# Weight slabs of the last two groups: asked for on ScalarE's queue instead of SyncE's

## The chip, the cores and the metric

The kernel runs on one core of a Trainium2 chip. Its time is the device time of one execution in microseconds (us). The time before is 1066.16 us, the median of 3 runs (1065.87 to 1067.72).

Engines go by their short names: PE is TensorE (matmuls; PEld its weight loads), DVE VectorE, ACT ScalarE, POOL GpSimd, SP SyncE. SP does no arithmetic here: it only sends out DMA transfers. ACT and POOL can send out transfers too, in order with their other work.

## The reference

Two blocks follow each other. All is fp32, with batch 8, 8 heads, 576 tokens and head size 64, so a row has 512 numbers.

```python
# attention inside chunks of 64 tokens
scores = (1 / sqrt(64)) * q_c @ k_c.T
attn = exp(scores - max(scores)); attn = attn / (sum(attn) + 1e-9)
x = attn @ v_c                        # then heads joined: (8, 576, 512)
# mixing by a Fourier transform over tokens and over columns, then an MLP
u  = x + real(fft(fft(x, axis=1), axis=2))
un = (u - mean(u)) / sqrt(var(u) + 1e-6)
out = u + relu(un @ w_ch1) @ w_ch2    # 512 -> 2048 -> 512
```

## The kernel before, in words

**Groups.** The 4608 rows (8 batches of 576) make 36 tiles of 128 rows, and the MLP takes them four at a time: nine groups, 0 to 8. Attention and the Fourier mixing of the next batch are woven into the MLP of the running group. Group 8 holds the four tiles with what is left of each batch, and has no attention beside it. `mlp(g)` runs the first product (512 to 2048, "up") and then the second one (2048 to 512, "down").

**Fewer multiplications.** From group 1 on the products are done by schemes that trade multiplications for sums. `up_halves` works on a pair of 128-column blocks of the result at a time, four pairs a group. A pair takes seven turns instead of eight, each one a smaller product of the weights' sums with the rows' sums; a turn is eight matmuls of 128x256, for two blocks r = 0 and 1. The turns follow `UP`. What becomes of a turn's result in PSUM (banks `pa` and `pb`) is written behind it: ACT copies the second turn's result (L1306) and DVE adds it to the first (L1307); DVE adds others (L1309, L1313, L1319, L1322); ACT applies the relu (L1317, L1320, L1323).

**The second product of the last two groups.** `down_few` (groups 7 and 8) has a list `PRODUCTS` of 26 small products, eight matmuls L1419 each, in place of 32. POOL sums operands between them (L1199, in `sums`), DVE adds results to the output rows (L1429).

**Weights.** The sums of weights are made once and kept in scratch tensors in HBM: `s1` for the first product, `s2` and `s3` for the second. From there they come back as slabs. A first-weight slab is 256 KB and goes to one of ten places in `wa` (`slab1`). A second-weight slab of `down_few` is 512 KB and goes to one of ten places (`slab3`): six in `wb`, two in rows of `xall` that are no longer needed, two in tiles called `more`. The contents of `s3` are made while group 6 ends and group 7 begins: the generator `make_rest` loads parts (L1137), POOL and DVE add them (L1148), and SP stores the results (L1155).

**Who asks for a slab, and when.** `fetch(which)` sends out the next slab of its kind, counted by `n_slab`. In the kernel before all go through SP's queue. First-weight slabs (L1171): ten ahead, and then one behind each turn of `up_halves`, into the place that this turn has just read; so the transfer waits for that turn's matmuls. The 28 slabs of a group (four pairs of seven) are asked for ten turns ahead of their use: in group 7 its slabs 10 to 27 and group 8's first ten, in group 8 the last 18. Second-weight slabs of groups 7 and 8 (L1174): in group 7 the first ten at fixed steps of the first product, as their places and contents come free (the `count` line in the main loop), and then one behind each small product. SP's queue also holds `make_rest`'s loads and stores and the stores of output rows (L1054; the low tiles go through POOL's queue, L1043).

**Order.** Each engine works its instructions off in order. The framework deals eight completion semaphores in turn to all transfers that SP and ACT send out, in the order in which it schedules them, and lets a transfer wait until the one that had the semaphore before it has landed.

Of the kernel before, what the change touches and what calls it, by code (L numbers as in the profile page):

```python
# [16 lines left out]
def kernel(  # L17
# [32 lines left out]
    nc = tc.nc  # L50
# [52 lines left out]
    NO, HF = 7, KF // 2  # L103
    UP = (1, 0, 2, 3, 4, 6, 5)
    s1 = dram.tile([HF // 2, NO, 128, 2 * 2 * 128], FP32, name="s1")
    s2 = dram.tile([NO, 128, HF * HM], FP32, name="s2")
    NS1, NS2, Z1, Z2 = 10, 3, 2 * 2 * 128, HF * HM
    slab1 = [wa[:, i * Z1:(i + 1) * Z1].rearrange("p (k r f) -> p k r f", r=2, k=2) for i in range(NS1)]
# [11 lines left out]
    PRODUCTS = (  # L120
        ("a41", "b11", "c", "+41", "a41=a22+a42 a22=a21-a22 a21=a41-a21"),
        ("a44", "b42", "b", "+42", "a44=a24+a44 a31=a21+a31"),
        ("y0", "s8", "d", "+12", ""),
        ("y3", "s21", "c", "+31+32+42", "y3=a43-y3"),
        ("y1", "s0", "d", "+11+21", "y1=a44-y1 y1=y1-a23 y0=a12-y0"),
        ("a22", "sb22", "f", "-22", "a22=a32-a34 a32=a42-a32"),
        ("a23", "s19", "d", "+22", ""),
        ("a44", "s15", "b", "+41", ""),
# [26 lines left out]
    NR2, NS3 = len(PRODUCTS), 10  # L155
# [952 lines left out]
    def block_of(name):  # L1108

        if name[0] == "s":  # L1110
            return s3[STORED.index(name)]
        o, k = (2, "dw".index(name)) if name in "dw" else ({"b1": 0, "b2": 0, "b3": 4 + "12".index(name[2]), "b4": 4 + "12".index(name[2])}[name[:2]], (int(name[1]) - 1) % 2)
        return s2[o, :, k * Z3:(k + 1) * Z3]
# [49 lines left out]
    FEW = NG - 2  # L1163
# [3 lines left out]
    def fetch(which):  # L1167
        i = n_slab[which]
        if which == 1 and i < HF // 2 * NO * (NG - 2):
            pair, o = divmod(i % (HF // 2 * NO), NO)  # L1170
            nc.sync.dma_start(out=slab1[i % NS1].rearrange("p k r f -> p (k r f)"), in_=s1[pair, UP[o]])  # L1171
        elif which == 3 and i < NR2 * (NG - FEW):
            to = slab3[i % NS3].rearrange("p m e -> p (m e)")
            nc.sync.dma_start(out=to, in_=block_of(PRODUCTS[i % NR2][1]))  # L1174
        elif which == 2 and i < NO * (FEW - first_of[2]):
            nc.sync.dma_start(out=slab2[i % NS2].rearrange("p m e -> p (m e)"), in_=s2[i % NO])
        n_slab[which] = i + 1
# [102 lines left out]
    def up_halves(g):  # L1280
# [4 lines left out]
        for pair in range(HF // 2):  # L1285
            pas, pbs = {}, {}
            for turn_, o in enumerate(UP):
# [36 lines left out]
                if g > 1:  # L1324
                    fetch(1)
# [7 lines left out]
    def down_halves(g, h1):  # L1333
        pas, pbs = {}, {}
        for o in range(NO):
            w = slab2[((g - first_of[2]) * NO + o) % NS2]
            for r in range(2):
# [45 lines left out]
                if r == 1:  # L1383
                    if o == 1:
                        for j in range(0, HF, 2):
                            two = ys[:, j:j + 2]
                            nc.gpsimd.tensor_tensor(
                                out=two, in0=h1[:, HF + j:HF + j + 2, lo], in1=two, op=ALU.subtract
                            )
                    if o == 2:  # L1390
                        for i in range(2):
                            nc.gpsimd.tensor_tensor(
                                out=os_[:, 2 * i + 1, HM:DM], in0=tmp[:, i, 0],
                                in1=natural(groups[g][2 + i])[:, HM:DM], op=ALU.add,
                            )
                    fetch(2)
                yield

    def down_few(g, h1):
# [3 lines left out]
        for o, (a, _, bank, reads, then) in enumerate(PRODUCTS):  # L1403
# [19 lines left out]
            for sign_, i, j in zip(reads[0::3], reads[1::3], reads[2::3]):  # L1423
# [7 lines left out]
                if left[i] == 0:  # L1431
                    store(n, os_[:, i])
            sums(h1, then.split())
            fetch(3)
            if o % 2 == 0:
                continue
# [14 lines left out]
    with tc.manual_schedule():  # L1451
# [79 lines left out]
        for g in range(NG):  # L1531
            for _ in mlp(g):
# [51 lines left out]
                for _ in range(2 if t > begin[1] else 0):  # L1584
                    if put_off:
                        b, t0_, r, o = put_off.pop(0)
# [60 lines left out]
```

## Time and profile before

| | |
|---|---|
| median of 3 runs | 1066.16 us (1065.87 to 1067.72) |
| profiled execution | 1065.92 us |
| its span, first to last instruction | 1064.1 us |
| PE busy | 1043.1 us (98%) |
| DVE, POOL, ACT busy | 627.6, 433.3, 314.9 us |
| first product of group 7 begins (PE) | 868.67 us |
| second product of group 7 begins | 917.86 us |
| first product of group 8 begins | 966.52 us |
| second product of group 8 begins, PE ends | 1015.0, 1059.9 us |
| SP's waits for PE ahead of L1171 and L1174, whole run | 81.7 + 42.3 and 49.6 us |

Times inside the profile count from the span's start. A timeline row gives the start, the duration, engine, line and operation, what it writes and reads, the shapes and how many instructions it joins; in brackets stands how long the engine was idle before it and what ended that. "SPq" and "ACTq" are transfers being sent out; their duration is that of the sending, not of the transfer. A row of the chain of waits that begins with DMA gives the time from sending to landing. The clock that the throttle granted to PE was 0.998 of full speed over the span.

### The profile page before, as it was taken

Reading aid. Unit: us, or ns where it says so; the run is one execution under the profiler, and the core shown is the slowest. Engines: PE = TensorE matmul, PEld = TensorE weight load, DVE = VectorE, ACT = ScalarE, POOL = GpSimd, SP = SyncE. Lnnn points to the kernel's source line nnn. Section 1 sums busy time; section 2 is a strip of 40 time slices with the busy share of each in tenths; the row PEclk is TensorE's granted clock in tenths of the full one; section 3 lists DMA queues with packets and bytes.
Section 4 is the critical chain, followed back from the end, with each engine's and each line's share of the span. In section 5 each row is a group of like instructions: output and inputs, shape, how many; then the busy total and the mean of one; then the engine's idle time right before and its main releaser. Section 6 shows DMA issues by size and latency. Waiting matters only on the chain.

```text
span 1064.1 us, 20223 instructions
## 1 busy us (share of the span) xinstructions
PE 1043.1 (98%) x7482; PEld 852.0 (80%) x7482; DVE 627.6 (59%) x1339; ACT 314.9 (30%) x744; POOL 433.3 (41%) x555
## 2 busy tenths in 40 slices
PE   8999998899999999999999999999999999999998
PEld 6645454788888888888888888888888888888887
DVE  4798987774567465664565645745664666433332
ACT  4688563233113311332022312331133102101210
POOL 4310018753425151244134421614251777650282
PEclk9999999999999999999999999999999999999999
DMA  8767575778478447973687359944753759998364
GB/s 178 223 199 215 146 217 199 208 231 294 161 217 238 128 146 213 242 211 111 186 235 212 113 170 231 246 132 159 228 158 103 271 174 356 348 407 280 90 213 143
DMA packets 167088, 219.10 MB, mean 206 GB/s; under 512 B 77228, under 2 KB 111020, under 8 KB 161614
## 3 DMA queue, kind: packets, MB, share of 16 engines
q1 hardware_dynamic: 155978, 211.98, 64.3%
q0 software_dynamic: 9024, 4.91, 2.1%
q8 instruction: 60, 0.98, 0.4%
q10 hardware_dynamic: 1988, 0.92, 0.3%
q14 instruction: 38, 0.31, 0.1%
HBM read 183.61 MB, written 34.08 MB: 205 GB/s over the span
## 4 chain that ended last, share of the span: by engine, by line
PE 79%; DVE 7%; ACT 4%; DMA 4%; SPq 3%; issue 1%; POOL 1%; ACTq 0%; DVEq 0%; POOLq 0%
PE pa L1301 20%; PE pb L1355 15%; PE pb L1301 15%; PE pa L1355 12%; PE dn L1419 7%; PE pt L399 2%; PE mix L839 2%; PE z L722 1%; PE xp L501 1%; SPq L265 1%; PE sc L451 1%; DMA s<-part 1%; DMA xall<-in_moe_w_ch_dram 1%; DVE power L380 1%; DMA more<-s 1%
## 5 line engine op out<-in xcount | busy, mean ns | idle before, releaser
L1301 PE MATMUL pa<-unT,wa 128*128 128x256 f32 x736 | 175.1, 381 | 0.0
L1301 PEld LDWEIGHTS pa<-unT,wa 128*128 128x128 f32 x736 | 138.1, 190 | 19.4 <-DVE h L1319 0.4
L1301 PE MATMUL pb<-wa 128*128 128x256 f32 x448 | 106.6, 381 | 0.0
L1301 PEld LDWEIGHTS pb<-wa 128*128 128x128 f32 x448 | 84.3, 190 | 11.5
L1355 PE MATMUL pa<-wb,h 128*128 128x256 f32 x384 | 87.2, 380 | 0.0
L1355 PE MATMUL pb<-wb,h 128*128 128x256 f32 x384 | 86.4, 379 | 0.0
L1185 POOL TENSOR_TENSOR h<-h 128x256 f32<-128x256 f32 x48 | 40.8, 857 | 101.2 <-DVE wb L1183 91.7
L1355 PEld LDWEIGHTS pa<-wb,h 128*128 128x128 f32 x384 | 71.8, 190 | 9.7
L1355 PEld LDWEIGHTS pb<-wb,h 128*128 128x128 f32 x384 | 72.0, 190 | 9.4
L1043 POOL DMA_DIRECT2D out_dram<-wb x28 | 18.8, 674 | 122.8 <-DVE wb L1372 71.9
L1307 DVE TENSOR_TENSOR wa<-pb,wa 128x256 f32<-128x256 f32 x56 | 23.7, 424 | 63.1 <-ACT wa L1306 63.1
L1301 PE MATMUL pb<-unT,wa 128*128 128x256 f32 x256 | 60.6, 379 | 0.3 <-DVE wa L1307 0.3
L1317 ACT ACTIVATE h<-pa 128x256 f32<-128x256 f32 x64 | 24.5, 383 | 114.8 <-PE pa L1301 114.3
L1252 PE MATMUL dn<-wb,h 128*128 128x512 f32 x128 | 57.4, 596 | 0.0
L1306 ACT COPY wa<-pa 128x256 f32<-128x256 f32 x56 | 20.8, 372 | 121.2 <-PE pa L1301 121.2
L1301 PEld LDWEIGHTS pb<-unT,wa 128*128 128x128 f32 x256 | 48.6, 190 | 7.2 <-DVE wa L1307 0.7
L1199 POOL TENSOR_TENSOR h<-h 128x512 f32<-128x512 f32 x34 | 43.0, 1280 | 27.1 <-ACT h L1323 23.9
L1301 PE MATMUL pa<-wa 128*128 128x256 f32 x224 | 53.9, 383 | 0.0
L1323 ACT ACTIVATE h<-h 128x512 f32<-128x512 f32 x64 | 39.8, 629 | 42.6 <-DVE h L1322 42.2
L483 ACT COPY pT<-pt 128x512 f32<-128x512 f32 x36 | 20.9, 581 | 105.8 <-PE pt L399 105.5
L1211 PE MATMUL up<-unT,wa 128*128 128x512 f32 x108 | 49.4, 598 | 0.0
L856 POOL TENSOR_TENSOR xall<-y,xall 128x513 f32<-128x513 f32 x14 | 22.7, 1620 | 62.3 <-DVE y L850 48.1
(312 smaller groups left out, 2139.6 us busy)
## 6 DMA issues: line engine op xcount, KB each, us to landing
wa<-s SPq DMA_DIRECT2D x196, 256.0 KB
wb<-s SPq DMA_DIRECT2D x42, 1024.0 KB
wb<-s SPq DMA_DIRECT2D x32, 512.0 KB
xall<-in_moe_w_ch_dram SPq DMA_DIRECT2D x22, 512.0 KB
q<-in_q_dram SPq DMA_DIRECT2D x96, 112.0 KB
k<-in_k_dram SPq DMA_DIRECT2D x96, 112.0 KB
s<-part SPq DMA_DIRECT2D x32, 256.0 KB
v<-in_v_dram SPq DMA_DIRECT2D x124, 64.0 KB
```

Source lines behind the costliest of these rows:

```text
L399: nc.tensor.transpose(pt[:, j, :], src(j), ident)
L856: eng.tensor_tensor(out=x[:, 0:w], in0=y[:, 0:w], in1=x[:, 0:w], op=ALU.add)
L1185: nc.gpsimd.tensor_tensor(out=h1[:, m, hi], in0=h1[:, m, lo], in1=h1[:, m, hi], op=ALU.subtract)
L1199: eng.tensor_tensor(out=out_, in0=a, in1=b, op=op)
L1211: nc.tensor.matmul(out=up, lhsT=w1[:, kk, m * 128:(m + 1) * 128], rhs=unT[:, kk], start=(kk == 0), stop=(kk == KD - 1), skip_group_check=True,
L1252: nc.tensor.matmul(out=dn, lhsT=h1[:, m, s * 128:(s + 1) * 128], rhs=w2[:, m, :], start=(m == 0), stop=(m == KF - 1),)
L1301: nc.tensor.matmul(out=dst, lhsT=w[:, kk, r], rhs=rhs[o][:, kk], start=(o in (0, 1) and kk == 0), stop=(kk == 1), skip_group_check=True,)
L1307: nc.vector.tensor_tensor(out=b, in0=pbs[r][:, 0], in1=a, op=ALU.add)
L1317: nc.scalar.activation(out=h1[:, m, lo], in_=dst, func=ACTF.Relu)
L1323: nc.scalar.activation(out=h1[:, HF + m], in_=h1[:, HF + m], func=ACTF.Relu)
L1355: nc.tensor.matmul(out=dst, lhsT=lhs[:, m], rhs=w[:, m], start=(o in (0, 2) and m == 0), stop=(m == HF - 1), skip_group_check=True,)
L1419: nc.tensor.matmul(out=dst, lhsT=lhs[:, m], rhs=w[:, m], start=(fresh and not half and m == 0), stop=(m == 3), skip_group_check=True,)
```

## The change

Which engine sends out a slab now depends on its number. First-weight slabs from number 150 on go through ACT's queue (`HF // 2 * NO * (FEW - 2) + NS1` is 28 x 5 + 10): that is each one asked for from the first turn of group 7 on, 46 in all. Second-weight slabs from number 10 on go through ACT's queue too, 42 in all; the first ten, those asked for during group 7's first product, stay with SP. Each `fetch` stands at the same place in the program, so ACT sends a slab out between the copies and activations that are written before and after it. The semaphores are dealt anew, as the scheduler now orders two queues.

```diff
         i = n_slab[which]
         if which == 1 and i < HF // 2 * NO * (NG - 2):
             pair, o = divmod(i % (HF // 2 * NO), NO)
-            nc.sync.dma_start(out=slab1[i % NS1].rearrange("p k r f -> p (k r f)"), in_=s1[pair, UP[o]])
+            eng = nc.scalar if i >= HF // 2 * NO * (FEW - 2) + NS1 else nc.sync
+            eng.dma_start(out=slab1[i % NS1].rearrange("p k r f -> p (k r f)"), in_=s1[pair, UP[o]])
         elif which == 3 and i < NR2 * (NG - FEW):
             to = slab3[i % NS3].rearrange("p m e -> p (m e)")
-            nc.sync.dma_start(out=to, in_=block_of(PRODUCTS[i % NR2][1]))
+            eng = nc.scalar if i >= NS3 else nc.sync
+            eng.dma_start(out=to, in_=block_of(PRODUCTS[i % NR2][1]))
```

## The prediction

> **What bounds the kernel now.** I read the busy times first, then the waits of each engine, then stretches of the last 250 us.
>
> ```profile
> PE 1043.1 (98%) x7482; PEld 852.0 (80%) x7482; DVE 627.6 (59%) x1339; ACT 314.9 (30%) x744; POOL 433.3 (41%) x555
> ```
>
> TensorE (PE) is busy for 98% of the span: 21 us of idle time in all, most of it in the opening. Up to group 7 (its first product begins at 868.67 us) the two programs stand in the same order, so only what follows can change. The stretches (length, then PE, PEld, DVE, ACT, POOL busy, clock, share of the DMA engines, GB/s):
>
> ```profile
> 872.00:876.00 4.00, 3.71 (x18) 2.97 (x17) 3.67 (x6) 0.37 (x1) 1.36 (x2) 1.00 0.46 138
> 875.00:935.00 60.00, 59.02 (x271) 50.71 (x269) 32.84 (x63) 13.26 (x30) 41.67 (x31) 1.00 0.96 350
> 905.00:910.00 5.00, 4.98 (x24) 4.07 (x23) 4.55 (x7) 1.63 (x5) 4.32 (x3) 1.00 0.71 264
> 910.00:915.00 5.00, 5.00 (x25) 4.41 (x24) 1.95 (x5) 0.77 (x2) 0.09 (x1) 1.00 0.82 258
> 920.00:925.00 5.00, 5.00 (x25) 4.38 (x24) 1.08 (x4) 0.00 (x0) 4.84 (x4) 1.00 1.04 404
> 967.00:1015.00 48.00, 48.00 (x224) 42.27 (x223) 16.70 (x40) 13.86 (x31) 9.40 (x10) 1.00 0.44 133
> 1015.00:1060.00 45.00, 44.92 (x209) 39.20 (x207) 12.14 (x31) 0.56 (x2) 26.86 (x22) 1.00 0.61 202
> ```
>
> Group 8 (967 to 1060) leaves nothing to win: PE full, DMA half empty. The only late weights are in group 7, whose 60 us run the DMA engines at 0.96. Its second product, PE alone in order of time:
>
> ```profile
> 926.50 1.89 PE L1419 MATMUL dn<-wb,h 128*128 128x256 f32 x8
> 928.38 3.69 PE L1419 MATMUL dn<-xall,h 128*128 128x256 f32 x16
> 932.11 1.97 PE L1419 MATMUL dn<-more,h 128*128 128x256 f32 x8
> 935.22 1.97 PE L1419 MATMUL dn<-more,yall 128*128 128x256 f32 x8 [1.15 <-DMA more<-s]
> 937.06 1.97 PE L1419 MATMUL dn<-wb,yall 128*128 128x256 f32 x8
> ```
>
> Eight matmuls make one small product, and where nothing is late one follows another every 1.727 us. From 926.50 to 937.06 there are five, 8.63 us of work in 10.56: PE loses **1.93 us** to slabs 6 to 10, of which the wait view books 1.15. Why they are late is seen in the chain of waits and in SyncE's (SP's) order of time:
>
> ```profile
> 913.78 5.91 DMA s<-part
> 919.75 6.93 DMA s<-part
> 928.09 6.99 DMA more<-s
> ```
> ```profile
> 869.33 5.30 SPq L1054 DMA_DIRECT2D out_dram<-wb  x4
> 877.18 0.90 SPq L1171 DMA_DIRECT2D wa<-s  x2
> 879.11 1.83 SPq L1171 DMA_DIRECT2D wa<-s  x2
> 881.26 3.37 SPq L1155 DMA_DIRECT2D s<-part  x4
> ```
>
> One queue holds the first-weight slabs (L1171), the stores of sums that POOL is making (L1155) and the second-weight slabs (L1174). The fetch that PE releases at 870.4 goes out at 877.18, behind stores. Fetch 27 is released at 917.9 and goes out at 928.6. Slab 9, the last of those that stay on SP, goes out at 928.09 and lands 6.99 us later.
>
> **The change, part by part.** 88 transfers leave SP for ScalarE (ACT): 28 first-weight fetches in group 7's first product, 18 in group 8's, 26 second-weight fetches in group 7's second product, 16 in group 8's. Nothing is added or dropped on PE, DVE or POOL. Semaphores matter, though. Eight are dealt in turn to every transfer of SP and ACT, and a transfer first waits until the one eight before it has landed. SP's transfers now wait for ACT's and the reverse; the engine stands in order behind each wait.
>
> *SP's queue.* In 869 to 929 it loses 28 issues of 0.375 us (median of L1171), 10.5 us, and their waits for PE. Stores and slabs move up. How far, the DMA engines decide: idle are about 2.2 us in 872 to 876, and 1.45 + 0.9 us in 905 to 915. So slabs 6 to 10 can land about 4.5 us earlier. They need 1.9 us at most: the loss goes, **-1.9 us**. Bounds: 0 (the queue is no faster) and -1.93. What is late next is DVE's L1307, which holds PE for 0.29 us at 874.31 and stays. The rows speak against more: at a share of 1.04 a second queue brings no bytes. The Trainium skill (DMA: Bandwidth & Descriptors, Issuing engines are not separate DMA queues) goes further: transfers of all issuers share 16 engines, so a second issuer saves its issue time alone. Taken strictly it leaves the slabs late and the sum 1.9 us higher. The idle shares, 0.71 and 0.82 ahead of the slabs, are why I don't follow it that far.
>
> *ACT's queue in group 7.* 28 x 0.375 + 26 x 0.32 us (medians) is 19 us of issuing on an engine that is busy for 13.26 of 60 us: beside other work. What counts is which ACT work stands behind a held fetch. In every pair of blocks (seven turns of 1.73 us) it is the copy L1306:
>
> ```profile
> 883.04 1.89 PE L1301 MATMUL pa<-unT,wa 128*128 128x256 f32 x8
> 884.11 0.37 ACT L1306 COPY wa<-pa 128x256 f32<-128x256 f32 x1 [1.64 <-PE pa L1301]
> 884.77 1.89 PE L1301 MATMUL pa<-wa 128*128 128x256 f32 x8
> ```
>
> The next turn writes the PSUM tile that this copy reads and waits for it. The copy ends at 884.48, PE goes on at 884.77: 0.29 us of slack, no more. The fetch ahead of it is released at about 883.2, so it may end as late as 884.4. Of the four pairs:
> - Pair 0 (fetch 0): the transfer eight before has long landed, so only the issue counts, 0.32 to 1.88 us (fastest and slowest L1171). At the slow end the copy ends at 872.8, PE starts late by 0.7 us and gets 0.45 back, as it stood for L1307. 0 to 0.3; I take 0.2, as SP's four stores at 869.33 took 1.3 us each.
> - Pair 1: fetch 7 waits for the first of the four stores at 881.26. With the four fetches (2.73 us) gone from ahead of it that goes out at 878.5, lands 4.6 (the landing there, by the semaphore's updates) to 6.99 us later, 883.1 to 885.5. 0 to 1.5; I take 0.4, nearer the landing at that place.
> - Pair 2: fetch 14 waits for fetch 10, which ACT sends out at 890 to 891 (fetch 10 itself waits for fetch 7, out at 884) and which lands 5 to 7 us later, 895 to 898, against 896.1 that is in time. 0 to 1.9; I take 0.6.
> - Pair 3: fetch 21 waits for fetch 18, out at about 903.5, through the emptier stretch of 905 to 915: 908 to 910 against 908.4. 0 to 2.0; I take 0.3.
>
> Together **+1.5 us**, between 0 and 4.5 (a late pair makes the next less late, so the four ends don't add). The other ACT work has room: in pair 1 the first activation L1317 ends at 889.67 and PE wants its tile at 891.68, and no matmul of this product waits for L1320 or L1323. On the first fetch the Trainium skill has a harsher rule (Perfetto Trace Analysis, DMA Instruction — HWDGE): the descriptor generator is shared and locked, and the profiled issue contains the wait for it. Behind SP's store of 869.33 to 871.40 and one of 2.1 us, pair 0 would cost about 1.4 us in place of 0.2, the sum 1.2 us more; only the start, where both queues issued together, hints at it in the rows.
>
> *Group 7's second product.* ACT has two copies L1012 there, 20.55 and 14.05 us idle before them; the fetch ahead of each waits for a product that PE has left behind. Cover 14 us: 0. POOL's out stores have a queue of their own and pass nothing.
>
> *Group 8.* A transfer eight back is eight turns old, 13.8 us, against landings of 2 to 4 us; fetches are not held, and 0.375 us ends before the copy. 0; should the slow issue (1.88) fall ahead of a copy, 0.4 us. In its second product ACT is busy for 0.56 of 45 us: 0. The closing stores stay where they were: 0.
>
> Sum: 1065.92 (profiled execution; span 1064.1, 1.8 around it) - 1.9 + 1.5 = 1065.5. The median of the runs is 0.24 above that execution: **1065.8 us**, no change that shows, as 0.2% (2.1 us) is about what a measurement of this kernel can tell from none.
>
> **Rivals.**
> 1. *ACT becomes the gate* (slower). If landings stay at 6 to 7 us right through 880 to 912, pairs 1 to 3 each hold the copy by more than 1 us, PE stops four times in group 7, and DVE's adds behind the copy delay the sums that POOL stores, which the next fetch waits for. Upper end 4.5 us, and more with that loop: 1066.2 - 1.9 + 4.5 to 6 = 1068.8 to 1070.3. For it: share 1.01 to 1.06 in 885 to 905 and 0.29 us of slack. Against: SP's stores go out earlier. It decides from 4.0 us of copy delay.
> 2. *All slabs early, no copy held* (the most that can be won): 1066.2 - 1.9 - 0.2 = 1064.1. For it: the scheduler spreads the eight semaphores anew. Against: rows of 5.9 to 7.0 us.
> 3. *Slabs 6 to 10 stay late*: bytes bound group 7, nothing is won, copies cost 1.5: 1067.7. For it: 0.96 over 60 us. Against: 0.71 and 0.82 before the slabs.
>
> **How the numbers follow.** Forecast 0.52 (1064.6 to 1067.0), ACT as gate 0.26, full gain 0.12, slabs still late 0.10. Faster by over 0.2% needs below 1064.0: half of the full gain, 0.06. Slower needs above 1068.3: nearly all of the first rival and a third of the third, 0.28. The rest, 0.66, is within. The range goes from the full gain, 1064.0, to the upper part of the first rival, 1070.0.
>
> **What would show it.** Right: no wait for "more" at L1419 and 1.73 us a product from 926 on; SP's slab 9 out before 925; some tenths of idle PE before the third turn of each pair, with L1306 later than PE's block end. Wrong: PE idle in 868 to 918 for over 4 us with ACT behind a fetch; or the wait of 1.15 still there; or group 8 losing PE time, where I see no reason.

## The result and the profile after

The changed kernel takes 1074.96 us (median of 11 runs, 1070.12 to 1078.24) against 1066.62 us (median of 11, 1065.35 to 1068.30): a ratio of 1.007, 95% interval 1.0054 to 1.0087. That is 8.3 us slower by the medians, and outside the forecast range of 1064 to 1070. The profiled execution took 1075.93 us, with a span of 1074.1 us, 10.0 more than before.

First the busy times and PE's largest wait in the changed kernel (us in total, times, longest):

```profile
PE 1046.8 (97%) x7482; PEld 855.0 (80%) x7482; DVE 627.4 (58%) x1339; ACT 314.1 (29%) x744; POOL 432.6 (40%) x555
```
```profile
PE pa L1303 <- ACT wa L1308: 6.5, 2, 4.8
```

PE is busy 3.7 us longer with the same 7482 instructions, so some of them ran slower, and a wait of 6.5 us is new: PE for ACT's copy (L1308 is L1306 of before; lines behind the edit have moved by 1 or 2). PE's order of time shows both stops:

```profile
886.11 1.89 PE L1303 MATMUL pa<-unT,wa 128*128 128x256 f32 x8
892.82 3.78 PE L1303 MATMUL pa<-wa 128*128 128x256 f32 x8 [4.81 <-ACT wa L1308]
896.39 2.21 PE L1303 MATMUL pb<-unT,wa 128*128 128x256 f32 x8
...
917.43 1.89 PE L1303 MATMUL pa<-unT,wa 128*128 128x256 f32 x8
921.04 1.99 PE L1303 MATMUL pa<-wa 128*128 128x256 f32 x8 [1.72 <-ACT wa L1308]
```

Both are the third turn of a pair, the second and the fourth pair of group 7's first product. Eight matmuls take 1.89 us in this view; behind the first stop they take 3.78. The stretches around it (length, PE, PEld, DVE, ACT, POOL busy, clock, DMA share, GB/s) say why:

```profile
887.00:892.00 5.00, 1.00 (x5) 0.55 (x3) 0.00 (x0) 0.72 (x2) 2.50 (x3) 0.82 1.06 382
892.00:897.00 5.00, 4.18 (x10) 3.38 (x11) 3.33 (x6) 0.65 (x2) 3.34 (x3) 0.50 1.03 331
897.00:902.00 5.00, 5.00 (x25) 4.41 (x24) 1.33 (x4) 0.69 (x2) 0.77 (x1) 1.00 1.03 386
```

The granted clock fell to half 2.2 us into the stop of 4.81 us and stayed there for 6.83 us (890.21 to 897.04, from the trace's clock records). So for about ten matmuls after the stop most starts followed the last by 0.43 us in place of 0.216: another 2.2 us that no wait view books. ACT's order of time at that place, and the chain that leads there:

```profile
890.52 1.83 ACTq L1172 DMA_DIRECT2D wa<-s  x2
892.39 0.65 ACT L1308 COPY wa<-pa 128x256 f32<-128x256 f32 x2 [2.31 <-DMA s<-part]
```
```profile
872.57 7.49 DMA out_dram<-wb
...
880.12 5.60 DMA s<-part
...
885.79 6.17 DMA s<-part
...
892.02 0.33 ACTq L1172
...
892.39 0.38 ACT wa L1308
```

Read it from the bottom. The copy stands behind ACT's fetch 7, sent at 892.02. That fetch waited for a store of SP's that holds the same one of the eight semaphores (out at 885.79, landed 6.17 us later); this store for another one (5.60 us), and that one for a store of output rows (7.49 us). One semaphore's four transfers in a row are the chain. ACT itself had nothing to do. The second stop has another holder: fetch 21, ahead of that copy, waited for ACT's own fetch 18, which went out at 912.46 and landed 7.7 us later, by the semaphore's updates.

Since PE's 7482 matmuls stand in the same order in all these kernels, the n-th can be set against the n-th. Lateness of PE's starts against the kernel before, in us, by stretch (worked out from the two traces):

| | at the start of group 7 | first product | second product | rest | from group 7 on |
|---|---|---|---|---|---|
| changed kernel | +3.24 | +8.68 | -2.01 | 0.00 | **+6.67** |

The 3.24 us come at 160 to 210 us, in code that is the same in both; they are scatter between executions, which the kernel before has too (1063.6 to 1071.9 in a later series). The change itself costs 6.67 us in this execution. The second product did get its loss back:

```profile
938.41 1.89 PE L1421 MATMUL dn<-wb,h 128*128 128x256 f32 x8
940.14 3.62 PE L1421 MATMUL dn<-xall,h 128*128 128x256 f32 x16
943.60 1.89 PE L1421 MATMUL dn<-more,h 128*128 128x256 f32 x8
945.32 1.89 PE L1421 MATMUL dn<-more,yall 128*128 128x256 f32 x8
947.05 1.89 PE L1421 MATMUL dn<-wb,yall 128*128 128x256 f32 x8
```

From 938.41 to 947.05 are 8.64 us for five products, where it was 10.56: no wait for `more` is left.

### The profile page after: what moved, and what is told of

The parts are those of the page before. It is cut to its first block, busy times and chain, and to the rows that moved or that the text cites. A ratio compares the mean times of both kernels' runs of the same rounds, so it can differ in the third digit from the quotient of the medians.

```text
span 1074.1 us, 20224 instructions
## 1 busy us (share of the span) xinstructions
PE 1046.8 (97%) x7482; PEld 855.0 (80%) x7482; DVE 627.4 (58%) x1339; ACT 314.1 (29%) x744; POOL 432.6 (40%) x555
## 4 chain that ended last, share of the span: by engine, by line
PE 77%; DVE 7%; DMA 5%; ACT 4%; SPq 3%; issue 2%; POOL 1%; ACTq 0%; DVEq 0%; POOLq 0%
PE pa L1303 19%; PE pb L1357 16%; PE pb L1303 14%; PE pa L1357 12%; PE dn L1421 8%; PE pt L399 2%; DMA s<-part 2%; PE mix L839 2%; PE z L722 1%; PE xp L501 1%; SPq L265 1%; PE sc L451 1%; DMA xall<-in_moe_w_ch_dram 1%; DVE power L380 1%; DVE wb L379 1%
## 5 line engine op out<-in xcount | busy, mean ns | idle before, releaser
L1319 ACT ACTIVATE h<-pa 128x256 f32<-128x256 f32 x64 | 24.3, 384 | 119.1 <-PE pa L1303 92.0
L1308 ACT COPY wa<-pa 128x256 f32<-128x256 f32 x56 | 20.7, 373 | 122.9 <-PE pa L1303 103.5
L1303 PEld LDWEIGHTS pa<-wa 128*128 128x128 f32 x224 | 42.7, 195 | 13.8 <-ACT wa L1308 7.3
```

Of the source, the lines that this page charges most:

```text
L1303: nc.tensor.matmul(out=dst, lhsT=w[:, kk, r], rhs=rhs[o][:, kk], start=(o in (0, 1) and kk == 0), stop=(kk == 1), skip_group_check=True,)
L1319: nc.scalar.activation(out=h1[:, m, lo], in_=dst, func=ACTF.Relu)
```

## The experiments

In each, "from group 7 on" is that kernel's profile against the one of before, matmul by matmul, as in the table above; the ratio is of device times, with its 95% interval. All start from the changed kernel's `fetch` unless it says otherwise. Summary first (us):

| run | first product | second product | from group 7 on | ratio to before |
|---|---|---|---|---|
| e1: group 7's first-weight fetches alone on ACT | +9.12 | -2.01 | +7.11 | 1.0088 (1.0058 to 1.0118) |
| e2: all the others alone on ACT | -0.39 | +7.84 | +7.45 | 1.0073 (1.0046 to 1.0099) |
| e7: slabs 10 to 15 alone on ACT | -0.42 | +6.53 | +6.11 | 1.0080 (1.0056 to 1.0104) |
| e8: group 8's fetches and slabs from 16 on | -0.19 | +5.07 | +4.88 | 1.0050 (1.0030 to 1.0070) |
| e3: one fetch on ACT | -0.09 | -0.85 | -0.95 | 0.9994 (0.9978 to 1.0011) |
| e10: changed kernel, ten fetches put off | +5.53 | -2.01 | +3.53 | 1.0035 (1.0021 to 1.0049) |
| e5: changed kernel, copies on DVE | +10.84 | -2.01 | +8.84 | 1.0060 (1.0040 to 1.0080) |
| e6: changed kernel, 48 stores by POOL | +14.04 | -1.73 | +12.31 | 1.0137 (1.0107 to 1.0168) |
| e4, e9: kernel before, ten fetches put off | -0.42, -0.44 | -2.01 | -2.43, -2.45 | 0.9991 (0.9973 to 1.0009), 0.9994 (0.9976 to 1.0012) |

### e1 and e2: the change cut in two

```diff
-            eng = nc.scalar if i >= HF // 2 * NO * (FEW - 2) + NS1 else nc.sync
+            eng = nc.scalar if 0 <= i - (HF // 2 * NO * (FEW - 2) + NS1) < HF // 2 * NO else nc.sync   # e1
+            eng = nc.scalar if i >= HF // 2 * NO * (FEW - 2) + NS1 + HF // 2 * NO else nc.sync   # e2
...
-            eng = nc.scalar if i >= NS3 else nc.sync
+            eng = nc.sync   # e1; e2 leaves this line as in the changed kernel
```

> Only the 28 first-weight fetches asked for during group 7's first product go through ACT; everything else as in the kernel before. Theory A (in that product a fetch on ACT stands until the SP transfer eight places before it has landed, and the copy L1308 stands behind the fetch): all of the loss is here, 4 to 11 us over the kernel before, PE stopped at least twice ahead of a third turn of a pair (some 4 to 5 us in the second pair, 1 to 2 in the fourth), and the slabs 6 to 10 of the second product are still on time, -1.9 us. Theory B (the loss comes with group 8's fetches or with the second-weight slabs on ACT): within 1 us of the kernel before.

> The other 60 transfers go through ACT (group 8's fetches, the second-weight slabs from number 10 on), group 7's 28 first-weight fetches stay on SP. Theory A: no copy is held; the time is that of the kernel before within 1 us, and PE's wait of about 1.1 us for the tile 'more' in group 7's second product is still there, since SP's queue ahead of slabs 6 to 9 is as it was. Theory B: 4 us or more over the kernel before, PE idle in 935 to 1060.

Measured: e1 1075.45 us, e2 1074.57 us, beside 1066.11 us. e1 is as theory A has it, with the first relu (L1319) held too:

```profile
PE pa L1303 <- ACT wa L1308: 4.3, 2, 3.1
...
PE pa L1303 <- ACT h L1319: 2.4, 2, 1.4
```

e2 is not. No copy is held there, and yet it loses as much, in one stop of group 7's second product:

```profile
PE dn L1421 <- DMA xall<-s: 7.1, 1, 7.1
```
```profile
925.48 0.14 SPq L1155
925.62 0.05 issue
925.67 8.86 DMA xall<-s
```

The slab for `xall` (number 6) goes out on SP at 925.67, 4.6 us later than before at the same state of PE (921.55, less the 0.44 us by which PE was early here), and takes 8.86 us. So theory A explains one half of the change, and the other half has a cause of its own. The two losses don't add: in the changed kernel the first one makes PE 8.68 us late, and then no slab is missing. On the clock of PE's start of group 7 (each kernel's times less its lateness there; called PE's time below), ACT sends slab 10 at 928.47 in the changed kernel, behind SP's slabs 6 to 9 (921.65 to 925.14); in e2 it sends it at 919.39, ahead of them.

### e7 and e8: which of the others

```diff
-            eng = nc.scalar if i >= NS3 else nc.sync
+            eng = nc.scalar if NS3 <= i < NS3 + 6 else nc.sync   # e7, first weights all on SP
+            eng = nc.scalar if i >= NS3 + 6 else nc.sync   # e8, group 8's first weights on ACT as in e2
```

> All on SP's queue as before, but for six transfers: second-weight slabs 10 to 15, asked for behind the first six steps of group 7's second product, go through ACT. Theory O (they go out as early as PE allows, take places among the eight and bytes ahead of SP's slabs 6 to 9, which PE needs first): PE stops for 4 to 8 us ahead of the tile xall at about 928, the time is 4 to 9 us over the kernel before. Rival (it takes all 26 of group 7 or group 8's share): within 1 us of the kernel before, or a stop under 1.5 us.

> The rest of the same set: group 8's 18 first-weight fetches and the second-weight slabs from number 16 on go through ACT, everything up to slab 15 stays on SP. Theory O: no stop other than the kernel before has (about 1.1 us for 'more'), the time within 1 us of it. Rival (a second queue costs as such in this stretch): 3 us or more over it, PE idle in 940 to 1060.

Measured: e7 1074.73 us, e8 1072.15 us, beside 1067.00 us. Six transfers cost nearly as much as the whole change (6.11 us of 6.67). PE's order of time in e7, then SP's:

```profile
927.96 1.89 PE L1421 MATMUL dn<-wb,h 128*128 128x256 f32 x8
935.67 5.16 PE L1421 MATMUL dn<-xall,h 128*128 128x256 f32 x16 [5.82 <-DMA xall<-s]
```
```profile
922.05 5.43 SPq L1155 DMA_DIRECT2D s<-part  x2
927.53 1.71 SPq L1176 DMA_DIRECT2D xall<-s  x2
```

ACT is free, so it sends slab 10 as soon as PE has left its place (921.25 in e7's trace; on SP it went out at 929.54, behind slab 9). In the deal of the semaphores it now stands ahead of SP's last stores: the second of the two stores in the row of 5.43 us waits for slab 10 to land, and slab 6 waits behind that store. A transfer that PE needs later has overtaken one that it needs first. For e8 theory O expected nothing, and it was wrong; the rival's 3 us or more came. The cause lies one step on and is again the places among the eight. In the deal ACT's slabs 16 and 17 stand ahead of SP's slab 9, and slab 18 ahead of slab 10. So slabs 9 and 10 wait for the transfer that is only six sendings back (slabs 7 and 8), and go out 1.8 and 2.9 us later than before in PE's time.

```profile
937.39 1.97 PE L1421 MATMUL dn<-more,yall 128*128 128x256 f32 x8 [1.25 <-DMA more<-s]
942.00 3.31 PE L1421 MATMUL dn<-wb,yall 128*128 128x256 f32 x7 [2.64 <-DMA wb<-s]
```

### e3: one fetch at the place of the longest stop

```diff
-            eng = nc.scalar if i >= HF // 2 * NO * (FEW - 2) + NS1 else nc.sync
+            eng = nc.scalar if i == HF // 2 * NO * (FEW - 2) + NS1 + NO else nc.sync
...
-            eng = nc.scalar if i >= NS3 else nc.sync
+            eng = nc.sync
```

> One fetch alone goes through ACT: the one that stands ahead of the second pair's copies in group 7, the place of the longest stop (4.81 us). Here the transfer eight places before it is a fetch of SP that lands at about 882.7 in the times of the kernel before, ahead of the 883.2 at which PE releases the place. Theory A (what costs is the landing of the transfer eight before): PE's third turn of that pair starts less than 0.6 us late, the time is within 1 us of the kernel before. Theory C (a fetch ahead of the copy costs as such, by its sending or by its PE wait, whatever the semaphores): PE stops for 1 us or more at that place, as in the changed kernel.

Measured: 1066.66 us beside 1066.11 us. Fetch 7 goes out at 883.10 and the copy is in time (ACT's order, then PE's):

```profile
883.10 0.36 ACTq L1172 DMA_DIRECT2D wa<-s  x1
883.97 0.37 ACT L1308 COPY wa<-pa 128x256 f32<-128x256 f32 x1 [1.64 <-DMA wa<-s]
```
```profile
882.90 1.89 PE L1303 MATMUL pa<-unT,wa 128*128 128x256 f32 x8
884.63 1.89 PE L1303 MATMUL pa<-wa 128*128 128x256 f32 x8
```

Theory C falls. The same fetch at the same place costs nothing when the transfer that it waits for has landed in time. On the clock of PE's start of group 7 this fetch went out at 889.26 on SP before, at 888.78 on ACT in the changed kernel (892.02 less 3.24), at 888.42 in e1, and at 883.43 here.

### e10: the changed kernel with ten fetches put off

```diff
-                if g > 1:
+                if g > 1 and (g != FEW or pair * NO + turn_ < HF // 2 * NO - NS1):
                     fetch(1)
+                if g > FEW and (pair * NO + turn_) % 2 and pair * NO + turn_ < 2 * NS1:
+                    fetch(3)
...
-            fetch(3)
+            fetch(1 if g == FEW and o >= NR2 - NS1 else 3)
```

> The changed kernel (its queues) with the order of e4: ten first-weight fetches and their 2.6 MB leave group 7's first product. Theory A with D (a fetch on ACT is held by the transfer eight places before it, in the first two pairs already): the stop ahead of the second pair's third turn stays, 3 to 6 us and the slow matmuls behind it, the one in the fourth pair goes; 4 to 9 us over the kernel before. Rival (the fourth pair's ten fetches make the backlog that holds ACT): no stop over 1 us in the first product, within 2 us of the kernel before.

Measured: 1070.25 us beside 1066.57 us. The second pair still stops, for a little less than the 3 us of theory A with D (and the time is 3.7 us over, just under its 4); the fourth doesn't:

```profile
890.46 2.41 PE L1303 MATMUL pa<-wa 128*128 128x256 f32 x8 [2.93 <-ACT wa L1308]
```

So the first stop doesn't need the ten fetches, and the second one did. The first product still costs 5.53 us.

### e5: the copies on DVE

```diff
-                        nc.scalar.copy(a, dst)
+                        if g == FEW:
+                            nc.vector.tensor_copy(out=a, in_=dst)
+                        else:
+                            nc.scalar.copy(a, dst)
```

> The changed kernel with one edit: in group 7 the copies L1308 are made by DVE, so nothing that PE's next turn waits for at once stands behind ACT's fetches. Theory D (two losses of which the first hides the second: ACT's held copies in the first product, and in the second product slabs 6 to 9 on SP overtaken by the slabs from number 10 on, which ACT sends out earlier): the waits for L1308 go from 6.5 to under 1 us, the relu L1319 may hold PE for 1 to 3 us, and now the second product stops for 3 to 7 us at a slab in 'xall' or 'more'; the time stays 3 to 9 us over the kernel before. Theory A alone (ACT's copies are all of the loss): no stop of over 1.5 us in the second product, the time within 2 us of the kernel before.

Measured: 1073.93 us beside 1067.00 us. ACT's copies are out of it (DVE's own first copy is late once, for 1.86 us), and the longest stop has moved to the next work on ACT, the first relu (L1322 in this kernel's lines is L1319 of the changed one). PE, then ACT:

```profile
896.96 3.78 PE L1303 MATMUL pa<-unT,wa 128*128 128x256 f32 x8 [4.97 <-ACT h L1322]
```
```profile
886.93 9.49 ACTq L1172 DMA_DIRECT2D wa<-s  x5
896.53 0.66 ACT L1322 ACTIVATE h<-pa 128x256 f32<-128x256 f32 x2 [10.57 <-DMA wa<-s]
```

Five fetches take ACT 9.49 us, far more than the 2 us of room that this relu has. Theory D's stop in the second product didn't come; PE was 9 us late again. That e2's loss is hidden rather than absent rests on e2 and e7 and on the order of sending given there. It isn't the copy that ACT's queue costs, but whatever ACT does next.

### e6: SP's stores out of the shared semaphores

```diff
-                    nc.sync.dma_start(out=block_of(old)[:, part], in_=where[old])
+                    nc.gpsimd.dma_start(out=block_of(old)[:, part], in_=where[old])
```

> The changed kernel with the 48 stores of make_rest (L1155) sent out by POOL, whose transfers have semaphores of their own. The bytes stay the same; what leaves is SP's stores from the eight semaphores that SP and ACT share. Theory R (ACT's fetch is held by the transfer eight places before it, mostly a store of SP's backlog): the waits for L1308 in the first product fall from 6.5 to under 1.5 us. Theory W (transfers land late because the DMA engines are full, through whatever queue): L1308 still holds PE for 4 us or more. In the second product POOL now has 0.67 us more per store, so its sums and with them the slabs can be late there; the total is put at 1066 to 1076 by R, 1072 to 1080 by W.

Measured: 1082.21 us beside 1067.00 us. The waits for L1308 are gone altogether, with the same bytes to move, as theory R has it; the total is above both ranges, for other waits take their place:

```profile
PE pb L1303 <- DVE h L1324: 4.6, 1, 4.6
...
PE pa L1303 <- ACT h L1319: 2.9, 2, 2.0
```

DVE now waits for POOL's stores before it can reuse their places (once for 7.15 us). It is also slower where POOL's adds and sendings follow one another: L1031, 1.41 and 1.38 us at its two places there before, takes

```profile
859.62 3.59 DVE wa L1031
```

This speaks for SP's stores among the eight as what held the copies, but not by itself: PE was already over 7 us late from the other waits at the second pair's third turn, which gives transfers more time to land. What shows it is the chain in the changed kernel's trace, together with e3. How much would be saved without the stores among the eight stays open.

### e4 and e9: what would have helped

The edit of e10, on the kernel before, with every slab on SP.

> The kernel before, all on SP's queue, with the order of needs changed: the last ten first-weight fetches of group 7's first product, which bring group 8's first slabs, are put off to the last ten steps of group 7's second product; the ten second-weight fetches that stood there (group 8's) go to every second turn of group 8's first product. If the lateness of slabs 6 to 10 is SP's queue and the 2.6 MB that those ten fetches bring into it ahead of slab 9: the wait for 'more' is gone, slab 9 goes out 4 us earlier or more, 1.9 us less than before, 1064 to 1065.5. If POOL's sums or their stores set when slabs 6 to 9 can go: the wait stays, within 0.5 us of before. If the ten fetches now come too late for group 8: PE idle near 967 or 1015, slower by 1 us or more.

> The same kernel as in e4 (all on SP, group 8's first ten slabs put off to the end of group 7's second product), for its time alone: from group 7 on its profile was 2.4 us shorter than that of the kernel before, while the total scattered by several us in both kernels. If those 2.4 us are there in every execution: a ratio of 0.9965 to 0.9990. If the profile was a lucky one: 0.9990 to 1.0010.

Group 8's first ten slabs (2.6 MB) are asked for in group 7 ahead of slabs that PE needs over 30 us sooner. Put off, they leave the second product without a loss; slab 9 goes out 4.5 us earlier in PE's time:

```profile
929.26 1.89 PE L1421 MATMUL dn<-wb,h 128*128 128x256 f32 x8
930.99 3.62 PE L1421 MATMUL dn<-xall,h 128*128 128x256 f32 x16
934.44 1.89 PE L1421 MATMUL dn<-more,h 128*128 128x256 f32 x8
936.17 1.89 PE L1421 MATMUL dn<-more,yall 128*128 128x256 f32 x8
```

Both profiles are shorter from group 7 on, by 2.43 and 2.45 us. The times don't show it: 1065.75 against 1066.11 us and 1065.61 against 1066.57 us, twelve runs each, with 1 in both intervals. Part of the reason is that the time outside the span rose, from 1.82 us (median of the runs of before beside e4) to 2.4 us; why is open. This is a gain in the trace that the measurement doesn't confirm, and the nearest thing to a version better than both kernels.

## Why the prediction was wrong

**What bounds the kernel.** Right: PE bounds it, and nothing before group 7 or in group 8 was touched. The lateness is constant from the last small products of group 7 on.

**SP's queue, -1.9.** The size came (-2.01), but by luck: the working failed. It counted 28 sendings of 0.375 us as time won. Sending was mostly not what SP waited for. In the 52 us from 8.3 us after group 7's start SP sent 63 transfers before, and SP and ACT together send 64 in the changed kernel; 39 and 40 of them left within 0.2 us of the landing of the transfer that had their semaphore before. Fetches that move to ACT still take places among the eight, so SP's stores are no earlier. Slab 9 went out 2.95 us earlier in PE's time (925.14 for 928.09), not 4.5; and as PE was 8.68 us late, the gain in the second product can't be credited to the queue. Here the Trainium skill (DMA: Bandwidth & Descriptors, Issuing engines are not separate DMA queues), which gives a second issuer its issue time and no more, was nearer to what the runs show than the reading that set it aside.

**ACT's queue, pair 1: the step that failed.** "With the four fetches (2.73 us) gone from ahead of it that goes out at 878.5": the store that fetch 7 waits for went out at 882.55 in PE's time (885.79 less 3.24), 1.3 us later than before instead of 2.8 earlier, because it stood for the landing of two stores before it (7.49 and 5.60 us), not for sendings. In the kernel before it did so too: it left 0.06 us after the load that had its semaphore, out at 876.15, had landed at 881.20. Its own landing, 6.17 us, lay inside the bounds used (4.6 to 6.99), though the 4.6 is misread. In the kernel before, that store's semaphore gets 16 updates from 885.70 to 887.50, and the fetch behind it went out after the last, so the landing took 6.24 us. So the term of 0.4 us, at most 1.5, was 4.81 us. That the copy has 0.29 us of room, that the fetch ahead of it decides, and at which store: all that was right.

**What had no term.** PE's granted clock. The stop of 4.81 us cost another 2.2 us behind it, and neither forecast nor rivals priced that.

**The other pairs.** Pair 0: 0.2 forecast, nothing lost; ACT's sending at 873.84 took 0.36 us, while four stores of SP took 5.87 us. The harsher rule on a shared descriptor generator, which would have made it 1.4 us, did not show on ACT. Pair 2: 0.6 forecast, no stop. Pair 3: 0.3 forecast, bound 2.0, measured 1.72; its gate was the one named, fetch 18, with a landing of 7.7 us where the working had at most 6.5.

**Group 7's second product and group 8 on ACT, 0 and 0.** The second product's 0 is wrong as a step, though the changed kernel hides it: e2, e7 and e8 lose 5.1 to 7.8 us there when PE is on time, because ACT's slabs take places ahead of SP's. The text looked for ACT work behind a held fetch and didn't ask what SP's slabs would wait for. Group 8's 0 came: PE's lateness no longer changes there in any run. (The landings of 2 to 4 us that it rests on hold from 978.8 us on; the first six of that group's fetches took 9.5 to 4.3 us.)

**The rivals.** What happened is the first one, ACT as the gate, at its place and by its mechanism, though PE stopped twice for a copy and not four times; its price, 4.5 to 6 us, was too small by the clock and by pair 1. The sign that was named beforehand, PE idle for over 4 us in 868 to 918 with ACT behind a fetch, is there.

## What to carry to other kernels

Before moving transfers to a second queue, find what releases each one on the first. If it is the landing of the transfer some fixed number of places before it, the new queue inherits the old one's backlog, and an engine that computes must not stand in it. And a queue that is free sends early what is needed late: put the urgent slabs first, or take what isn't needed yet out of their way, before adding a queue.

## What the runs showed of the hardware

- After a longer stop PE ran at half clock for a while. Stops of 1.72 us (changed kernel) and 1.86 us (e5) left the next matmuls at 0.216 us from start to start; after stops of 2.04 and 4.56 (e6), 2.64 (e8), 2.93 (e10), 3.07 (e1), 4.81 (changed kernel), 4.97 (e5), 5.82 (e7) and 7.11 us (e2), 5 to 13 matmuls went at 0.43 us, which cost 1.5 to 3.2 us more each time. The granted clock stood at half for 3.41 or 6.83 us each time, by the clock records. In e1 and e10 the slow ones began only 1.0 to 1.4 us after PE had started again. The Trainium skill (TensorE: Matmul & The Clock Gate, Part 1: The HAM clock gate) has a free-running window of about 3.4 us and half clock after one idle window; the two lengths and the late beginning agree with a free-running window, but here 2.0 to 2.9 us of standing were enough, so the measurement decides.
- Two halves of an edit that cost 7.11 and 7.45 us alone cost 6.67 us together. A profile of the whole change would have shown one cause only.
- Executions of the same code differ by -1.4 to +4.6 us at the start of group 7 (all profiles but e6's, whose edit begins earlier), which is as much as the effects here. Setting the n-th matmul against the n-th from that point on gave the same 2.43 and 2.45 us twice where the total gave 0.36 and 0.96.
